# Squares of raw weight blocks moved within a token tile, and the last pair's output products put off for four halves instead of three

## The chip, the cores and the metric

The kernel runs on one core of one Trainium2 chip. The metric is the device time of one execution in microseconds. Three runs of the kernel before gave 1804.94, 1809.9 and 1811.93 us; their median, 1809.9 us, is the time before. The profiled execution of it took 1808.81 us, with a span of 1807.0 us between its first and last instruction.

## The reference, cut to what matters

```python
h = _layernorm(x) * (1 + ca) + sa
x = x + ga * _A_ref(h, ...)              # state space layer, first 450 us of the kernel
h = _layernorm(x) * (1 + cb) + sb
# _B_ref, gated MLP: S = 2048 tokens, D = 576, Fh = 2304
z  = gelu(h @ w_in)                      # (S, 2*Fh)
z1 = z[..., :Fh]
z2 = _layernorm(z[..., Fh:])
g  = einsum("ts,sf->tf", w_sp, z2) + b_sp[:, None]
x  = x + gb * ((z1 * g) @ w_out)         # w_out: (Fh, D)
```

All matrix products are made in parts of half precision: a factor is scaled by a power of two, rounded to a high part, and its remainder is kept as a low part; three products of these parts (high by high, high by low, low by high) are added in PSUM. The scales come from the sums of squares of the raw weights. That is what the squares in this change are for.

## The kernel before, in words

**First part (to about 440 us).** The state space layer `ssm`. The change doesn't touch it.

**Phase A (`phase_a`, about 440 to 702 us).** Sixteen tiles of 128 tokens, called token tiles here, b = 0 to 15. Each makes the second half of z: five groups of 14 matmuls (`z2_mm`, columns 512h to 512h+511) into PSUM tiles `pz`, gelu on ScalarE (`z2_gelu`), the statistics on VectorE (`z2_stats`, `roots`), the normalization on ScalarE (`z2_norm`, one tile late), and a store to DRAM from GpSimd (`z2_store`). The z tile has two buffers, so the first gelu of tile b waits until the store of tile b-2 has landed. The transposed rows `nt` of the next tile are split by ScalarE (`turn_hi`) and VectorE (`turn_lo`); TensorE starts a tile when its `nt` is there.

Every engine here keeps the order in which the code is written. The main work stands in that order by hand, and side work is hung into it: `side(b, k, fn, ...)` puts a call at place k of tile b. The places that matter are, in the order of one tile: LD (loads, at the start), A0 (ScalarE, after the first group of matmuls and ahead of the first gelu of the tile), PE, V0, A1 (after the third gelu, ahead of the fourth), V1 (ahead of the last group). The side work is

- `side_load`, `side_sum`, `side_hi`, `side_lo`: the first half of w_in, one column block q in two token tiles; its sum of squares stands at A0 of the odd tiles, and a small matmul at PE (`win_scale`) needs it.
- `wsp_load`, `out_load`: raw blocks of w_sp and w_out (26 in all, two in a tile, 512 KB or 432 KB each) into the tile `wsst`, which has two buffers; `norm_sp`, `norm_out`: ScalarE squares such a block in place and adds up the squares into a column of `acc`. A load into a buffer waits until the block before in it has been squared.
- from tile 9 on, `block_load`, `wsp_sums`, `wsp_hi`, `wsp_lo`: blocks 0 to 6 of w_sp for the first output quarter, through a single buffer `xz`: load at V1 of a tile, sums on VectorE at V0 of the next, high parts on ScalarE at A1, low parts on VectorE at V1, then the next load into the buffer.

In the code before, the loads of a pair of raw blocks stand at A1 of tile b, and their squares at A0 of tile b+1.

**Phase B (`phase_b`, about 702 us to the end).** Four quarters q of 512 output tokens. In each, 18 units of z1 (`z1_unit`), nine units of g (`g_unit`, f = 0 to 8; `g_products` runs 168 matmuls into four PSUM banks, VectorE combines them into `gt`, multiplies with z1, and ScalarE and VectorE split the product into `prods[q, f]`), then `out_block(q)`. For q < 3 the eight w_sp blocks of the next quarter are built ahead of `out_block` in the code (`wsp_build`: four subtractions L1001 to L1004 and two low parts L787 on VectorE, two high parts L781 on ScalarE, for each block). Here VectorE, ScalarE and TensorE are not held to the written order: when the program is built, a scheduler sets the order of each engine's queue by its own estimates, and the order stays fixed after that.

`out_block(q)` makes eight halves (tt, h): 128 tokens by 288 columns, called h0 to h7 below. Each takes two of the eight PSUM banks, `pa` and `pl`, and adds over nine f and two k, three matmuls each: 54 matmuls, six of them for f = 8. Since `prods[q, 8]` comes last, h0, h1 and h2 first run f = 0 to 7, 48 matmuls each; then the six of f = 8 follow for each of the three. `out_sum` empties a half: ScalarE reads `pl` into `ot` (L1431), VectorE adds `pa` (L1432), multiplies (L1433) and adds the residual rows (L1434). h4 is the first half that takes banks which an earlier half has used.

Of the kernel before, what the change touches and what calls it, by code (L numbers as in the profile page):

```python
# [752 lines left out]
class Mlp:  # L753
# [418 lines left out]
    def phase_a(self):  # L1172
# [13 lines left out]
        LD, PE, A0, A1, V0, V1 = range(6)  # L1186
        sides = [[[] for _ in range(6)] for _ in range(17)]

        def side(b, k, fn, *a):
            sides[b][k].append((fn, a))  # L1190
# [13 lines left out]
        for h in range(2):  # L1204
            side(1, LD, self.bsp_load, ap, h)
            side(2, A0, self.norm_bsp, h)
        for i in range(8):
            side(2 + i // 2, A1, self.wsp_load, 0, i, ap)
            side(3 + i // 2, A0, self.norm_sp, 0, i)
        for i in range(12):  # L1210
            side(6 + i // 2, A1, self.out_load, ap, i)
            side(7 + i // 2, A0, self.norm_out, i)
        for i in range(6):
            side(12 + i // 2, A1, self.wsp_load, 1, i, ap)
            side(13 + i // 2, A0, self.norm_sp, 1, i)
        side(13, V1, self.sums_out)
        side(14, PE, self.scales_out)
        side(6, V1, self.sums_sp, 0)
# [217 lines left out]
    def out_block(self, q):  # L1436

        nc = self.nc
        A, S = nc.scalar, nc.sync
        halves = [(tt, h) for tt in range(4) for h in range(2)]  # L1440
        xts, pms = {}, {}
        for n, (tt, h) in enumerate(halves):
            if h == 0:
                xts[tt] = self.raw(("x", tt)).rearrange("p k n -> p (k n)")[:, :D]
                S.dma_start(xts[tt], self.x1_d[4 * q + tt])
            pms[tt, h] = [self.bank()[:, :288] for _ in range(2)]
            self.out_products(pms[tt, h], q, tt, h, range(8) if n < 3 else range(9))
            for k in range(3) if n == 2 else () if n < 2 else (n,):
                tt, h = halves[k]
                if n == 2:  # L1450
                    self.out_products(pms[tt, h], q, tt, h, (8,))
                self.out_sum(pms[tt, h], xts[tt], q, h)
                b, hs = 4 * q + tt, slice(288 * h, 288 * h + 288)
                if b == 15:
                    (A, S)[h].dma_start(self.out[b, :, hs], xts[tt][:, hs])
                elif h == 1:
                    A.dma_start(self.out[b], xts[tt])
# [170 lines left out]
```

## Time and profile before

| what | value |
|---|---|
| median of 3 runs | 1809.9 us (1804.94 to 1811.93) |
| profiled execution | 1808.81 us, span 1807.0 us |
| TensorE (PE) busy | 1696.9 us, 94% of the span |
| VectorE (DVE) busy | 1120.0 us, 62% |
| ScalarE (ACT) busy | 786.0 us, 43% |
| mean granted TensorE clock | 0.984 of full |

PE, DVE, ACT, POOL and SP are the engines TensorE, VectorE, ScalarE, GpSimd and SyncE. A row of the timeline gives start, duration, engine, source line, operation, output and inputs; brackets at its end give the idle time of that engine just before it, and what ended it. Instructions of phase A all carry the line of the helper that records them, L129, and are told apart by their tiles. A busy PE is one with a matmul in flight; matmuls overlap, so a matmul of 0.29 us can start 0.12 us after the one before it.

### The profile page before, as it was taken

What the parts mean: (1) busy time and instruction counts of PE and PEld (TensorE: products, weight loads), DVE (VectorE), ACT (ScalarE), POOL (GpSimd) and SP (SyncE); (2) the same over time, 40 slices, a digit from 0 to 9 for tenths busy, and PEclk for the clock granted to TensorE, in tenths of its full rate; (3) what the DMA queues carried; (4) which work ended last, traced back from release to release, by engine and by line L of the source; (5) the groups of instructions that cost most, each with busy time, mean ns of one, the idle gap of its engine ahead of it and who ended that gap; (6) DMA issues with size and microseconds to landing.
All of it is one profiled execution on the core that took longest, in us unless ns stands there. A gap on an engine that the chain in (4) does not pass through costs nothing.

```text
span 1807.0 us, 34140 instructions
## 1 busy us (share of the span) xinstructions
PE 1696.9 (94%) x14226; PEld 1198.7 (66%) x14226; DVE 1120.0 (62%) x2240; ACT 786.0 (43%) x1021; POOL 227.4 (13%) x358
## 2 busy tenths in 40 slices
PE   3768899997899999999999999999999999999998
PEld 1334555565455544877777778777788777887787
DVE  5787999966988997999685443474222365222322
ACT  3758999944566666555442222242111132011110
POOL 3121222332122211000000000000000000000000
PEclk9988999998999999999999999999999999999999
DMA  7565736679688788887563766572655572455520
GB/s 215 164 183 199 205 110 168 184 205 295 203 259 265 243 247 237 300 291 268 187 228 111 268 243 220 195 262 95 216 187 204 179 263 68 168 181 180 198 82 27
DMA packets 160122, 361.57 MB, mean 200 GB/s; under 512 B 23040, under 2 KB 76800, under 8 KB 158816
## 3 DMA queue, kind: packets, MB, share of 16 engines
q1 hardware_dynamic: 118944, 166.75, 30.4%
q0 software_dynamic: 33536, 155.05, 25.6%
q10 hardware_dynamic: 7488, 37.60, 5.1%
q8 instruction: 111, 1.82, 0.4%
q14 instruction: 43, 0.35, 0.1%
HBM read 256.86 MB, written 93.05 MB: 194 GB/s over the span
## 4 chain that ended last, share of the span: by engine, by line
PE 49%; DVE 17%; DMA 9%; issue 4%; ACT 3%; POOL 0%; SPq 0%; ACTq 0%; DVEq 0%; POOLq 0%
PE ps L1338 9%; PE ps L1373 8%; PE ps L1375 8%; PE ps L1374 8%; PE ps L1422 3%; PE ps L1424 3%; PE ps L1423 3%; DVE zset L1057 3%; DMA raw<-in_w_spT 3%; DVE gt L1387 2%; DMA z_d<-z 2%; PE pz L129 2%; DVE bsz L129 1%; DMA gbs<-in_w_out 1%; ACT z L129 1%
## 5 line engine op out<-in xcount | busy, mean ns | idle before, releaser
L1373 PE MATMUL ps<-wsp,zset 128*128 128x256 f16 x2016 | 550.7, 273 | 2.4 <-DVE gt L1387 2.4
L1375 PE MATMUL ps<-wsp,zset 128*128 128x256 f16 x2016 | 550.8, 273 | 1.1 <-DVE zset L1057 1.1
L1374 PE MATMUL ps<-wsp,zset 128*128 128x256 f16 x2016 | 550.6, 273 | 0.0
L129 PE MATMUL pz<-wz,nt 128*128 128x512 f16 (+1 forms) x1120 | 226.4, 362 | 10.5 <-ACT nt L129 4.5
L1387 DVE SCALAR_TENSOR_TENSOR gt<-ps,sc,bsp 128x512 f32<-128x512 f32 x36 | 27.0, 749 | 316.9 <-PE ps L1375 316.8
L1338 PE MATMUL ps<-n2q,wf 128*128 128x512 f16 x1008 | 223.1, 379 | 0.0
L1373 PEld LDWEIGHTS <-zset 128*128 128x128 f16 x2016 | 197.7, 98 | 29.1 <-DVE gt L1387 2.7
L1374 PEld LDWEIGHTS <-zset 128*128 128x128 f16 x2016 | 197.5, 98 | 26.5
L1375 PEld LDWEIGHTS <-zset 128*128 128x128 f16 x2016 | 197.5, 98 | 24.5 <-DVE zset L1057 1.4
L129 PEld LDWEIGHTS <-nt 128*128 128x128 f16 x1120 | 109.9, 99 | 118.5 <-issue 7.7
L1350 POOL DMA_DIRECT2D zset<-set_d x96 | 50.8, 529 | 972.1 <-PE ps L1375 758.9
L1338 PEld LDWEIGHTS <-wf 128*128 128x128 f16 x1008 | 98.6, 98 | 111.8
L1343 ACT ACTIVATE z<-ps,sc 128x512 f32<-128x512 f32 x56 | 37.8, 680 | 281.4 <-PE ps L1338 278.9
L1423 PE MATMUL ps<-wout,z 128*128 128x288 f16 x448 | 128.3, 286 | 0.1
L1424 PE MATMUL ps<-wout,z 128*128 128x288 f16 x448 | 128.3, 286 | 0.0
L1422 PE MATMUL ps<-wout,z 128*128 128x288 f16 x448 | 128.3, 286 | 0.0
L1387 DVE SCALAR_TENSOR_TENSOR gt<-ps,sc,gt 128x512 f32<-128x512 f32 (+1 forms) x180 | 122.0, 695 | 5.4
L1057 DVE TENSOR_TENSOR zset<-raw,zset 128x1024 f16<-128x1024 f32 x48 | 58.6, 1221 | 73.2 <-ACT zset L1056 73.2
L1056 ACT ACTIVATE zset<-raw 128x1024 f16<-128x1024 f32 x48 | 50.3, 1051 | 99.8 <-PE ps L1375 72.4
L129 ACT ACTIVATE z<-pz,sc 128x512 f32<-128x512 f32 (+1 forms) x80 | 49.8, 644 | 50.9 <-DMA z_d<-z 37.9
L1432 DVE TENSOR_TENSOR ot<-ot,ps 128x288 f32<-128x288 f32 x32 | 14.2, 453 | 82.7 <-ACT ot L1431 82.7
L1431 ACT ACTIVATE ot<-ps 128x288 f32<-128x288 f32 x32 | 12.7, 407 | 108.5 <-PE ps L1422 93.1
(310 smaller groups left out, 2854.7 us busy)
## 6 DMA issues: line engine op xcount, KB each, us to landing
zset<-set_d POOLq DMA_DIRECT2D x96, 896.0 KB, 4.9
set_d<-zset ACTq DMA_DIRECT2D x36, 896.0 KB, 5.9
raw<-z_d SPq DMA_DIRECT2D x48, 512.0 KB, 4.6
wf<-win_d SPq DMA_DIRECT2D x72, 320.0 KB, 3.4
raw<-in_w_spT SPq DMA_DIRECT2D x43, 512.0 KB, 6.3
z_d<-z POOLq DMA_DIRECT2D x32, 576.0 KB, 7.9
u_d<-st1o POOLq DMA_DIRECT2D x16, 576.0 KB, 3.9
u<-u_d SPq DMA_DIRECT2D x36, 256.0 KB, 5.2
```

The costliest lines, as they stand in the source:

```text
L129: return self.tc.keep_in_program_order(f(*a, **k))
L1056: nc.scalar.activation(o[:, k, 0], t, AF.Copy)
L1057: nc.vector.tensor_tensor(o[:, k, 1], t, o[:, k, 0], op=ALU.subtract)
L1338: nc.tensor.matmul(pm.rearrange("p (t c) -> p t c", t=4), w[:, kw], self.n2[q][:, :, kn], start=i == 0, stop=i == len(Z1) - 1)
L1350: self.nc.gpsimd.dma_start(o, self.set_d[n // 4, n % 4])
L1373: T.matmul(pm, z[:, a, 0, c], w[:, b, 0], start=i + half == 0, stop=False, skip_group_check=True)
L1374: T.matmul(pm, z[:, a, 0, c], w[:, b, 1], start=False, stop=False, skip_group_check=True)
L1375: T.matmul(pm, z[:, a, 1, c], w[:, b, 0], start=False, stop=i == 7, skip_group_check=True)
L1387: V.scalar_tensor_tensor(dst, pm, inv, to, op0=ALU.mult, op1=ALU.add)
L1422: T.matmul(pl, p[:, 1, ts], w[:, 0, hs], start=st, stop=sp)
L1423: T.matmul(pa, p[:, 0, ts], w[:, 0, hs], start=st, stop=False)
L1424: T.matmul(pa, p[:, 0, ts], w[:, 1, hs], start=False, stop=sp)
```

## The change

Two edits. In phase A the squares (`norm_sp`, `norm_out`) go from A0 of the token tile to A1 of the same tile, and are registered ahead of the loads, so that on ScalarE they follow the third gelu of a tile and stand ahead of `wsp_hi`, and each load is issued after the squares that free its buffer. In `out_block` four halves, h0 to h3, run f = 0 to 7 first; then f = 8 follows for these four. No instruction is added or taken away; the queues of GpSimd and SyncE keep their order.

```diff
@@ phase_a
         for i in range(8):
+            side(3 + i // 2, A1, self.norm_sp, 0, i)
+        for i in range(12):
+            side(7 + i // 2, A1, self.norm_out, i)
+        for i in range(6):
+            side(13 + i // 2, A1, self.norm_sp, 1, i)
+        for i in range(8):
             side(2 + i // 2, A1, self.wsp_load, 0, i, ap)
-            side(3 + i // 2, A0, self.norm_sp, 0, i)
         for i in range(12):
             side(6 + i // 2, A1, self.out_load, ap, i)
-            side(7 + i // 2, A0, self.norm_out, i)
         for i in range(6):
             side(12 + i // 2, A1, self.wsp_load, 1, i, ap)
-            side(13 + i // 2, A0, self.norm_sp, 1, i)
@@ out_block
             pms[tt, h] = [self.bank()[:, :288] for _ in range(2)]
-            self.out_products(pms[tt, h], q, tt, h, range(8) if n < 3 else range(9))
-            for k in range(3) if n == 2 else () if n < 2 else (n,):
+            self.out_products(pms[tt, h], q, tt, h, range(8) if n < 4 else range(9))
+            for k in range(4) if n == 3 else () if n < 3 else (n,):
                 tt, h = halves[k]
-                if n == 2:
+                if n == 3:
                     self.out_products(pms[tt, h], q, tt, h, (8,))
                 self.out_sum(pms[tt, h], xts[tt], q, h)
```

## The prediction

> **What bounds the kernel now.** I read the page first (busy shares, and the chain that ended last), then busy time by stretches, then TensorE's idle times and the timelines of ScalarE and VectorE around them.
>
> ```profile
> PE 1696.9 (94%) x14226; PEld 1198.7 (66%) x14226; DVE 1120.0 (62%) x2240; ACT 786.0 (43%) x1021; POOL 227.4 (13%) x358
> ...
> PE 49%; DVE 17%; DMA 9%; issue 4%; ACT 3%; POOL 0%; SPq 0%; ACTq 0%; DVEq 0%; POOLq 0%
> ```
> ```profile
> 487.00:605.00 118.00, 117.60 (x628) 61.84 (x627) 104.48 (x329) 80.37 (x123) 29.52 (x40) 1.00 0.78 250
> 605.00:702.00 97.00, 91.71 (x476) 46.81 (x475) 85.10 (x251) 63.50 (x89) 18.66 (x22) 0.98 0.81 247
> ```
> ```profile
> 960.00:1190.00 230.00, 230.00 (x1842) 179.93 (x1840) 101.17 (x163) 60.48 (x79) 11.63 (x22) 1.00 0.60 215
> ```
>
> The columns of the stretches are length, then busy time of PE, PEld, DVE, ACT and POOL. TensorE is the bound in the quarters of phase B (230.00 of 230) and in phase A up to tile 8 (117.60 of 118). From tile 9 on it is 5.3 us idle out of 97, and VectorE, 85.10 us busy there before the small gaps between its instructions are counted, sets the pace. So whatever makes TensorE wait in phase B is paid in full, and in the second half of phase A what delays VectorE is paid.
>
> **The output blocks.** TensorE's rows around the f = 8 products of the first three quarters; each stall ends with the last split of `prods[q, 8]` (L1403), and the rows without brackets are the last matmul ahead of the first stall and the second matmul of h4:
>
> ```profile
> 944.90 0.29 PE L1424 MATMUL ps<-wout,z1b 128*128 128x288 f16 x1
> 946.66 0.30 PE L1422 MATMUL ps<-wout,z1b 128*128 128x288 f16 x1 [1.47 <-ACT z1b L1403]
> ...
> 955.61 0.29 PE L1423 MATMUL ps<-wout,z 128*128 128x288 f16 x1
> ...
> 1219.97 0.30 PE L1422 MATMUL ps<-wout,z1b 128*128 128x288 f16 x1 [0.63 <-ACT z1b L1403]
> ...
> 1228.92 0.29 PE L1423 MATMUL ps<-wout,z 128*128 128x288 f16 x1
> ...
> 1494.49 0.30 PE L1422 MATMUL ps<-wout,z1b 128*128 128x288 f16 x1 [1.61 <-ACT z1b L1403]
> ...
> 1503.44 0.29 PE L1423 MATMUL ps<-wout,z 128*128 128x288 f16 x1
> ```
>
> What the edit removes: three waits, 1.47 + 0.63 + 1.61 = 3.7 us. With h3's 48 matmuls put in, TensorE reaches f = 8 some 5.9 us later than now (48 at 0.1226; from 946.66 to 955.61 are 73 starts), well after `prods` is there. In the last quarter there is no such stall and nothing to win.
>
> What it adds: h4 comes closer to the sums that free its banks. Before, between f = 8 of h0 and the start of h4 lay the 54 matmuls of h3, 6.6 us; after, only the f = 8 products of h1 to h3, 18 matmuls or 2.2 us. The sums of h0 wait in queues that hold w_sp builds. First ScalarE, then VectorE:
>
> ```profile
> 953.87 0.69 ACT L1431 ACTIVATE ot<-ps 128x288 f32<-128x288 f32 x2
> 956.28 1.15 ACT L781 ACTIVATE wsp<-sum,sc 128x1024 f16<-128x1024 f32 x1 [1.72 <-DVE sum L1004]
> ...
> 1229.59 1.15 ACT L781 ACTIVATE wsp<-sum,sc 128x1024 f16<-128x1024 f32 x1 [1.72 <-DVE sum L1004]
> ...
> 1504.11 1.15 ACT L781 ACTIVATE wsp<-sum,sc 128x1024 f16<-128x1024 f32 x1 [1.72 <-DVE sum L1004]
> ```
> ```profile
> 955.83 0.42 DVE L1004 TENSOR_TENSOR sum<-raw,sum 128x256 f32<-128x256 f32 x1
> 956.16 0.81 DVE L1432 TENSOR_TENSOR ot<-ot,ps 128x288 f32<-128x288 f32 x2
> ...
> 957.63 1.28 DVE L787 SCALAR_TENSOR_TENSOR wsp<-sum,sc,wsp 128x1024 f16<-128x1024 f32 x1
> ...
> 959.82 0.46 DVE L1432 TENSOR_TENSOR ot<-ot,ps 128x288 f32<-128x288 f32 x1 [0.17 <-ACT ot L1431]
> ```
>
> Before, ScalarE's two reads of `pl` (953.87) stand ahead of the last build (956.28); h4 takes the two `pl` banks that these reads free, at 954.56, and starts at 955.49 without waiting. In the order of the changed program both engines do the last build first: on ScalarE the last high part precedes all L1431, on VectorE the last low part L787 precedes the first L1432. And h4 takes `pl` and `pa` of h0, so its second matmul waits for VectorE's L1432. The time of that is fixed by VectorE, which is busy with builds without a break and sees nothing of the edit before this point: L1004 ends and releases ScalarE's last high part at 956.28 as now; this ends at 957.43; then L787 takes 1.28, to 958.71; then L1432 takes 0.46, to 959.17. TensorE's second matmul of h4 starts there instead of at 955.61: 3.6 us later. In the second quarter 1229.59 + 1.15 + 1.28 + 0.46 = 1232.48 against 1228.92, 3.6; in the third 1504.11 + 2.89 = 1507.00 against 1503.44, 3.6. This is net of the removed waits: **+10.7 us**. The last quarter has no builds in these queues; there h0's sums need 1.15 us (0.69 for two L1431, 0.46 for L1432) against 2.2 us of cover, so nothing. Cover gone, this would cost the 3.6 a fourth time.
>
> The new stall itself is 3.6 plus the old wait: 5.1, 4.2 and 5.2 us. Stalls of this length have a second price:
>
> ```profile
> 883.83 0.28 PE L1373 MATMUL ps<-wsp,zset 128*128 128x256 f16 x1 [2.38 <-DVE gt L1387]
> ```
> ```profile
> 885.40:888.80 3.40, 3.40 (x20) 2.48 (x18) 3.33 (x5) 0.69 (x1) 0.00 (x0) 0.54 0.82 319
> 888.80:893.00 4.20, 4.20 (x41) 3.77 (x39) 3.11 (x5) 2.08 (x3) 0.00 (x0) 1.00 0.23 96
> 945.00:950.00 5.00, 3.53 (x30) 2.68 (x29) 5.00 (x11) 2.75 (x3) 0.00 (x0) 1.00 0.19 59
> ```
>
> After an idle time of 2.38 us the granted clock (the column before the DMA share) fell to 0.54 for 3.4 us, in which 20 matmuls started; at the pace of the next stretch, 41 in 4.2 us, it would have been 33. The 13 missing cost 13 x 0.102 = 1.3 us; a whole such stretch at half rate costs 1.7. The stall of 1.47 us at 946.66 left the clock at 1.00. I take 1.6 us for each of three stalls, **+4.8 us**, nearest to the 2.38 us row. Bounds: nothing, if the dip falls inside the stall, and two stretches each, 3.2 x 3 = 9.6.
>
> The Trainium skill ("TensorE: Matmul & The Clock Gate", Part 1) has the clock halved only after at least one idle window of about 3.4 us of a free-running grid. By it a stall of 5.2 us holds a whole window in about half of its placements, and as an estimate from that page the three would cost about 2 us instead of 4.8. The row above speaks against it: 2.38 us, shorter than such a window, was enough here.
>
> **The squares.** Per tile ScalarE's work is the same; its place moves from a spot where ScalarE mostly waits anyway into the dense middle.
>
> ```profile
> ACT z L129 <- DMA z_d<-z: 37.9, 11, 6.6
> ```
> ```profile
> 625.45 1.80 ACT L129 ACTIVATE wsp<-xz,sc 128x1792 f16<-128x1792 f32 x1
> ...
> 670.96 1.80 ACT L129 ACTIVATE wsp<-xz,sc 128x1792 f16<-128x1792 f32 x1
> ...
> 674.96 1.06 ACT L129 ACTIVATE wsst<-wsst 128x1024 f32<-128x1024 f32 x1 [1.26 <-DMA wsst<-in_w_spT]
> ...
> 680.25 1.06 ACT L129 ACTIVATE wsst<-wsst 128x1024 f32<-128x1024 f32 x1 [4.15 <-DMA wsst<-in_w_spT]
> ...
> 700.76 1.78 ACT L129 ACTIVATE wsp<-xz,sc 128x1792 f16<-128x1792 f32 x1
> ```
> ```profile
> 628.65 2.03 DVE L129 SCALAR_TENSOR_TENSOR wsp<-xz,sc,wsp 128x1792 f16<-128x1792 f32 x1
> ...
> 672.98 2.08 DVE L129 SCALAR_TENSOR_TENSOR wsp<-xz,sc,wsp 128x1792 f16<-128x1792 f32 x1
> ...
> 685.25 1.10 DVE L129 TENSOR_TENSOR xz<-xz 128x256 f32<-128x256 f32 x3 [4.51 <-DMA xz<-in_w_spT]
> ...
> 702.57 2.08 DVE L129 SCALAR_TENSOR_TENSOR wsp<-xz,sc,wsp 128x1792 f16<-128x1792 f32 x1 [0.20 <-ACT wsp L129]
> ```
>
> What it removes: squares no longer hold ScalarE ahead of a tile's first gelu while their load is late (1.26 and 4.15 us in front of tile 14), and the loads, issued later in a tile, let the z2 store go first; ScalarE waits 37.9 us for such stores. Little of that is on the path from tile 9 on, where VectorE sets the pace. What it adds: `wsp_hi` comes two squares, 2 x 1.06 = 2.1 us, later, and VectorE's `wsp_lo` waits for it. In tile 10, `wsp_hi` ends at 627.25 and would end at 629.2 (the blocks of w_out are a little shorter), against 628.65: 0.6 us; tile 12 the same; tile 13, 672.8 + 2.1 = 674.9 against 672.98: 2.0. These 3.2 us run into VectorE's wait of 4.51 us for the `xz` load, where the load's slow landing beside the raw loads can take them up. Behind it, tile 14 pays up to 2.1, of which I count half, since ScalarE is no longer held until 681 ahead of that tile; tile 15 pays its 2.2 in full, as VectorE waits there for `wsp_hi` already. VectorE's delay passes to TensorE in the first quarter: the 2.38 us stall above, ended by VectorE, says that TensorE has no slack against it. I take 1.1 + 2.2 = **+3.3 us**. The upper bound counts 3.2 + 2.1 + 2.1 = 7.4; the lower is a gain, bounded by TensorE's waits of that stretch and the dip after the longest:
>
> ```profile
> PE pz L129 <- ACT nt L129: 3.8, 4, 2.1
> PE pz L129 <- DVE nt L129: 1.5, 1, 1.5
> ```
>
> 3.8 + 1.5 + 1.7 = 7.0 us. SyncE's later loads (w_in column blocks, `x1_load`) stand behind the raw loads and go later with them; they are used about a tile later (the 118.00 us stretch above is eight tiles, so 14.7 us), which hides it.
>
> **Sum.** 10.7 + 4.8 + 3.3 = 18.8 us on the profiled execution of 1808.81 us: 1827.6. That execution lies 1.1 us under the median; I predict **1828 us**.
>
> **Rivals.**
> - *The clock mostly holds.* Only one of the three stalls brings a dip that TensorE's work meets, the others none or one that ends inside the stall: 10.7 + 1.6 + 3.3 = 15.6, 1824 us. For it: 1.47 us left the clock alone. Against: 2.38 didn't. 0.13. The rule of the Trainium skill named above would lead here.
> - *Phase A gains what the output blocks lose.* The store waits and the late squares were what held ScalarE's `nt`, and with them gone all 7.0 us of TensorE's loss goes: 15.5 - 7.0 = 8.5, 1817 us. For it: 37.9 us of waiting; against: VectorE's queue has no room. 0.12.
> - *Phase A loses more.* The squares in tiles 4 and 6 push the w_in sums behind them, on which TensorE's scale matmuls wait (some 2 us), and all 7.4 us on VectorE are paid: 15.5 + 9.4 = 25, 1834 us. 0.11.
> - *Faster.* The banks of h4 come free in time: then 3.7 us of waits go at no price and up to 7.0 in phase A: 1798 us. It decides at L1432 of h0 ending before 953.9 (945.02 plus 72 matmuls); the queue orders put it at 959.2. 0.04.
>
> The forecast keeps 0.60.
>
> **How the numbers follow.** 0.5% of 1809.9 is 9 us, about what a measurement of this kernel can tell from no change. Slower by more: forecast, first and third rival, 0.84; within: second, 0.12; faster: 0.04. The low end, 1815, holds the second rival; the high end, 1837, is the three upper bounds together, 10.7 + 9.6 + 7.4 = 27.7. Both signs hardly meet here, so one range stands.
>
> **What would show it.** In the changed profile: no wait for L1403 in front of the f = 8 products; instead, in three quarters, a wait of 4 to 5 us in h4's first two matmuls, ended by L1432 or L1431; granted clock near 0.5 for some 3.4 us behind it; two squares between third and fourth gelu of a tile, and longer waits of VectorE for `wsp_hi` in tiles 13 to 15. I am wrong if h4 starts without a wait, or if phase A ends over 4 us earlier.

## The result and the profile after

| kernel | median | profiled execution | span | granted clock |
|---|---|---|---|---|
| before | 1809.4 us (4 runs, 1804.94 to 1811.93) | 1808.81 us | 1807.0 us | 0.984 |
| changed | 1832.8 us (4 runs, 1831.74 to 1833.97) | 1832.74 us | 1830.7 us | 0.979 |

The ratio is 1.0131, 95% interval 1.0106 to 1.0157: slower by 23.7 us (19.2 to 28.4), where 18.8 us were forecast. The predicted time was 1828, the range 1815 to 1837.

The page of the changed kernel: the busy line, and the groups of out matmuls that wait (busy us, mean ns; idle us before them and what ended it). The second and third lines of `out_products` are L1425 and L1426 now, and `out_sum` begins at L1434.

```profile
PE 1705.5 (93%) x14226; PEld 1201.5 (66%) x14226; DVE 1121.9 (61%) x2240; ACT 784.9 (43%) x1021; POOL 228.0 (12%) x358
...
L1425 PE MATMUL ps<-wout,z 128*128 128x288 f16 x448 | 129.6, 289 | 10.2 <-ACT ot L1434 10.2
L1426 PE MATMUL ps<-wout,z 128*128 128x288 f16 x448 | 129.7, 289 | 3.5 <-DVE ot L1435 3.2
```

10.2 + 3.2 us are new waits for the sums of the output halves; the waits for the last split of `prods[q, 8]` are gone.

Where the time went can be read from six marks. First, the timeline of the kernel before (on TensorE the five transposes that turn the rows of tile 2, which stand in tile 1; the first z2 store on GpSimd, the first matmul of phase B, the first and the last out matmul of the first quarter), then the same of the changed kernel, with the first and last out matmul of the last quarter.

```profile
486.83 0.71 PE L129 MATMUL pt<-ident,n 128*128 128x128 f32 x5
489.65 2.03 POOL L129 DMA_DIRECT2D z_d<-z  x2 [14.17 <-ACT z L129]
702.32 7.93 PE L1338 MATMUL ps<-n2q,wf 128*128 128x512 f16 x36
927.38 0.29 PE L1422 MATMUL ps<-wout,z 128*128 128x288 f16 x1
981.83 0.29 PE L1424 MATMUL ps<-wout,z1b 128*128 128x288 f16 x1
```
```profile
480.49 0.71 PE L129 MATMUL pt<-ident,n 128*128 128x128 f32 x5
485.93 2.04 POOL L129 DMA_DIRECT2D z_d<-z  x2 [14.16 <-ACT z L129]
707.42 2.75 PE L1341 MATMUL ps<-n2q,wf 128*128 128x512 f16 x12
936.53 0.29 PE L1425 MATMUL ps<-wout,z 128*128 128x288 f16 x1
996.39 0.29 PE L1427 MATMUL ps<-wout,z1b 128*128 128x288 f16 x1
...
1772.86 0.29 PE L1425 MATMUL ps<-wout,z 128*128 128x288 f16 x1
1825.66 0.29 PE L1427 MATMUL ps<-wout,z1b 128*128 128x288 f16 x1
```

| stretch | before | changed | difference |
|---|---|---|---|
| start to the first z2 store | 489.65 | 485.93 | -3.7 |
| first z2 store to phase B | 212.67 | 221.49 | +8.8 |
| phase B to the first out matmul | 225.06 | 229.11 | +4.1 |
| out block, first quarter | 54.45 | 59.86 | +5.4 |
| out blocks, second, third, last quarter | 53.60, 54.80, 52.79 | 56.80, 60.03, 52.80 | +8.4 |
| the three stretches between the blocks, and the end | 663.98 | 664.68 | +0.7 |
| span | 1807.0 | 1830.7 | +23.7 |

The first row isn't the edit's: no square moves before tile 3, and over the profiles of this study the first store lies between 485.7 and 490.1 us, the turn of tile 2 between 480.1 and 486.8. The output blocks cost 13.8 us. What phase A costs depends on the mark, since the first store is made by another engine than the rest, and a loss of phase A can also show behind it: the third stretch takes 223.4 to 229.1 us in these profiles. Counted on TensorE alone, from the turn to the first out matmul, the four profiles in which phase A isn't edited (before, experiments 1, 3 and 8) agree: 440.55, 441.61, 441.39 and 440.05 us. The changed kernel has 456.04. By this count the squares cost 15.5 us in this execution, and its earlier turn (480.49 against 486.83) gives 6.3 back. Of the 15.5 us TensorE loses 1.3 up to the turn of tile 6 and 7.9 from there to the turn of tile 8, then 2.2 up to phase B and 4.1 in phase B.

**Output blocks.** TensorE at the start of h4, all three stalls; then ScalarE and VectorE around the first:

```profile
966.90 0.40 PE L1425 MATMUL ps<-wout,z 128*128 128x288 f16 x1 [3.75 <-ACT ot L1434]
968.29 0.40 PE L1426 MATMUL ps<-wout,z 128*128 128x288 f16 x1 [0.99 <-DVE ot L1435]
...
1245.95 0.28 PE L1425 MATMUL ps<-wout,z 128*128 128x288 f16 x1 [2.58 <-ACT ot L1434]
1247.34 0.28 PE L1426 MATMUL ps<-wout,z 128*128 128x288 f16 x1 [1.10 <-DVE ot L1435]
...
1524.31 0.28 PE L1425 MATMUL ps<-wout,z 128*128 128x288 f16 x1 [3.90 <-ACT ot L1434]
1525.69 0.40 PE L1426 MATMUL ps<-wout,z 128*128 128x288 f16 x1 [1.10 <-DVE ot L1435]
```
```profile
965.41 1.15 ACT L781 ACTIVATE wsp<-sum,sc 128x1024 f16<-128x1024 f32 x1 [2.32 <-DVE sum L1004]
966.46 0.69 ACT L1434 ACTIVATE ot<-ps 128x288 f32<-128x288 f32 x2
```
```profile
966.59 1.28 DVE L787 SCALAR_TENSOR_TENSOR wsp<-sum,sc,wsp 128x1024 f16<-128x1024 f32 x1 [1.22 <-ACT wsp L781]
967.79 0.45 DVE L1435 TENSOR_TENSOR ot<-ot,ps 128x288 f32<-128x288 f32 x1
```

Each stall comes in two pieces: the read of `pl` frees the bank of the first matmul, L1435 that of the second, and each stands right behind the last build on its engine. The stalls are 4.7, 3.7 and 5.0 us. A block without any wait takes 52.80 us (last quarter: 1825.66 - 1772.86). The first has 59.86 - 52.80 = 7.06, so 2.3 us beside its stall; the second 4.00, 0.3 beside; the third 7.23, 2.2 beside. Most of that rest is the clock; 0.2 to 0.4 us of it the blocks of the kernel before, too, have beside their waits (54.45 - 52.80 - 1.47 = 0.18), and the third holds a wait of 0.34 us for `gt`. Two stretches after the first stall and one after the second (length; busy us and starts of PE, PEld, DVE, ACT, POOL; granted clock; DMA share; GB/s):

```profile
966.90:970.00 3.10, 2.11 (x9) 1.17 (x9) 3.03 (x7) 0.67 (x2) 0.00 (x0) 0.50 0.47 182
970.00:973.50 3.50, 3.50 (x22) 2.39 (x21) 2.89 (x7) 0.41 (x1) 0.00 (x0) 0.69 0.24 89
1245.90:1249.40 3.50, 2.35 (x18) 1.75 (x18) 3.43 (x8) 0.71 (x2) 0.00 (x0) 1.00 0.44 161
```

Read in steps of half a us, the clock fell while TensorE still stood in the first stall, at about 965.4, and was back at about 972.2: 6.8 us at half rate, 5.3 of them behind the first matmul of h4. Around the second stall it stayed at 1.00. At the third it fell at about 1525.1, for 3.4 us.

**Phase A.** TensorE's waits for the sums of w_in in tiles 5 and 7:

```profile
535.71 0.38 PE L129 MATMUL pz<-acc,ones 128*128 128x1 f32 x2 [1.17 <-ACT wso L129]
...
569.45 0.59 PE L129 MATMUL pz<-acc,ones 128*128 128x1 f32 x2 [5.01 <-ACT wso L129]
```

The same two matmuls in the kernel before:

```profile
540.73 0.38 PE L129 MATMUL pz<-acc,ones 128*128 128x1 f32 x2
...
569.86 0.38 PE L129 MATMUL pz<-acc,ones 128*128 128x1 f32 x2 [0.40 <-ACT wso L129]
```

What the wait in tile 7 is for, in the changed kernel on ScalarE and on SyncE, and SyncE of the kernel before:

```profile
549.78 1.06 ACT L129 ACTIVATE wsst<-wsst 128x1024 f32<-128x1024 f32 x1
...
566.97 2.34 ACT L129 ACTIVATE wso<-wst 128x2560 f16<-128x2560 f32 x1 [2.39 <-DMA wst<-in_w_in]
```
```profile
550.96 1.40 SPq L129 DMA_DIRECT2D wsst<-in_w_spT  x2
552.41 2.66 SPq L129 DMA_DIRECT2D wst<-in_w_in  x3
```
```profile
545.91 0.90 SPq L129 DMA_DIRECT2D wsst<-in_w_spT  x2
546.86 2.21 SPq L129 DMA_DIRECT2D wst<-in_w_in  x3
```

On SyncE the w_in load stands behind the raw loads. These now wait for the squares that free `wsst`, the first of which ends at 550.84; so the w_in load goes out at 552.41 instead of 546.86. It lands 12.7 us later, the sum of squares waits 2.39 us for it, TensorE 5.01 us for the sum, and then runs at a clock of 0.50 for two stretches of 3.4 us.

Measured against TensorE's own progress the load is later than that. It went out 6.1 us behind the scale matmul of tile 5 before (546.86 - 540.73) and goes out 16.7 us behind it now (552.41 - 535.71). TensorE was ready for the sum of tile 7 at 569.46 before and at 564.44 now. So the load had 22.6 us, and now has 12.0, less than the transfer alone takes.

From tile 9 on, VectorE's waits (in total, times, longest) and three of them in the timeline:

```profile
DVE xz L129 <- DMA xz<-in_w_spT: 8.7, 3, 5.1
DVE wsp L129 <- ACT wsp L129: 5.7, 5, 2.7
```
```profile
610.11 1.56 DVE L129 TENSOR_TENSOR xz<-xz 128x256 f32<-128x256 f32 x4 [2.21 <-DMA xz<-in_w_spT]
...
678.79 2.08 DVE L129 SCALAR_TENSOR_TENSOR wsp<-xz,sc,wsp 128x1792 f16<-128x1792 f32 x1 [1.75 <-ACT wsp L129]
...
711.63 2.08 DVE L129 SCALAR_TENSOR_TENSOR wsp<-xz,sc,wsp 128x1792 f16<-128x1792 f32 x1 [2.74 <-ACT wsp L129]
```

The forecast waits for `wsp_hi` in tiles 13 and 15 are there at 1.75 and 2.74 us (forecast 2.0 and 2.2). A wait for `xz` in tile 9, 2.21 us, is new and was not forecast. TensorE itself waits for ScalarE's `nt` from tile 11 on, 6.0 us in all against 3.8 before. ScalarE's waits for the z2 stores grew from 37.9 us to 60.6, the longest of them 8.4.

### The profile page after: what moved, and what is told of

The parts are those of the page before. It is cut to its first block, busy times and chain, and to the rows that moved or that the text cites. A ratio compares the mean times of both kernels' runs of the same rounds, so it can differ in the third digit from the quotient of the medians.

```text
span 1830.7 us, 34114 instructions
## 1 busy us (share of the span) xinstructions
PE 1705.5 (93%) x14226; PEld 1201.5 (66%) x14226; DVE 1121.9 (61%) x2240; ACT 784.9 (43%) x1021; POOL 228.0 (12%) x358
## 4 chain that ended last, share of the span: by engine, by line
PE 44%; DVE 16%; DMA 10%; issue 8%; ACT 4%; SPq 1%; POOL 0%; ACTq 0%; DVEq 0%; POOLq 0%
PE ps L1341 9%; PE ps L1376 8%; PE ps L1378 8%; PE ps L1377 8%; DVE zset L1057 3%; PE ps L1426 2%; DMA z_d<-z 2%; PE ps L1427 2%; PE ps L1425 2%; DMA raw<-in_w_spT 2%; DVE gt L1390 2%; PE pz L129 1%; DVE wsp L787 1%; ACT z L129 1%; DMA wst<-in_w_in 1%
## 5 line engine op out<-in xcount | busy, mean ns | idle before, releaser
L129 PE MATMUL pz<-wz,nt 128*128 128x512 f16 (+1 forms) x1120 | 229.1, 364 | 10.9 <-ACT nt L129 6.7
L1390 DVE SCALAR_TENSOR_TENSOR gt<-ps,sc,bsp 128x512 f32<-128x512 f32 x36 | 26.9, 748 | 317.0 <-PE ps L1378 316.8
L129 PEld LDWEIGHTS <-nt 128*128 128x128 f16 x1120 | 110.7, 100 | 120.7 <-issue 10.6
L1425 PE MATMUL ps<-wout,z 128*128 128x288 f16 x448 | 129.6, 289 | 10.2 <-ACT ot L1434 10.2
L1426 PE MATMUL ps<-wout,z 128*128 128x288 f16 x448 | 129.7, 289 | 3.5 <-DVE ot L1435 3.2
L1427 PE MATMUL ps<-wout,z 128*128 128x288 f16 x448 | 129.6, 289 | 0.0
L129 ACT ACTIVATE z<-pz,sc 128x512 f32<-128x512 f32 (+1 forms) x80 | 49.6, 644 | 69.4 <-DMA z_d<-z 60.6
L1435 DVE TENSOR_TENSOR ot<-ot,ps 128x288 f32<-128x288 f32 x32 | 14.4, 451 | 92.4 <-ACT ot L1434 92.4
L1434 ACT ACTIVATE ot<-ps 128x288 f32<-128x288 f32 x32 | 12.8, 408 | 120.6 <-PE ps L1425 110.2
```

The source lines that it names most:

```text
L129: return self.tc.keep_in_program_order(f(*a, **k))
L1390: V.scalar_tensor_tensor(dst, pm, inv, to, op0=ALU.mult, op1=ALU.add)
L1425: T.matmul(pl, p[:, 1, ts], w[:, 0, hs], start=st, stop=sp)
L1426: T.matmul(pa, p[:, 0, ts], w[:, 0, hs], start=st, stop=False)
L1427: T.matmul(pa, p[:, 0, ts], w[:, 1, hs], start=False, stop=sp)
```

## The experiments

Each was timed in five rounds beside the kernel before on its chip, whose median was 1805.2 (runs 1 to 4), 1806.1 (5 to 8) and 1806.2 us (9 to 11). Ratios are of the same chip, with 95% intervals; microseconds are the ratio times 1805. A profile is one execution: those of 2, 5 and 6 lie 7.5, 3.3 and 4.6 us under the median of their kernel and that of 9 lies 4.3 above, so their rows show which waits there are, and the medians what an edit costs.

**1. The output blocks' edit alone.** The second hunk of the diff, not the first:

```diff
-range(8) if n < 3 else range(9)
+range(8) if n < 4 else range(9)
-for k in range(3) if n == 2 else () if n < 2 else (n,):
+for k in range(4) if n == 3 else () if n < 3 else (n,):
```

> The output blocks' edit alone (four halves put off), the squares as before. My theory: three stalls of h4 on the sums of h0, net 3.6 us each after the removed waits for L1403, and dips of the clock of about 3.4 us in all (2.0 + 0 + 1.4, from the matmuls that ran at half rate in the changed kernel): 1809.4 + 10.7 + 3.4 = 1823.5 us, range 1820 to 1826, and phase A as in the kernel before (220 us from the first w_in scale group of tile 1 to the start of phase B). Rival 'the squares are harmless, the output blocks cost it all': 1833. Rival 'the loss sits in phase A': under 1815.

Ratio 1.0100 (1.0086 to 1.0115), +18.1 us (15.5 to 20.8). Phase A is 209.1 us, not longer than before. The three stalls are 4.9, 4.2 and 4.9 us. The second, and the first stretch behind it:

```profile
1233.46 0.40 PE L1422 MATMUL ps<-wout,z 128*128 128x288 f16 x1 [3.22 <-ACT ot L1431]
1234.85 0.40 PE L1423 MATMUL ps<-wout,z 128*128 128x288 f16 x1 [0.99 <-DVE ot L1432]
```
```profile
1233.40:1236.80 3.40, 2.35 (x10) 1.31 (x10) 3.33 (x7) 0.72 (x3) 0.00 (x0) 0.50 0.46 164
```

Here the second stall halved the clock too, from about 1232.4 to 1239.2. The blocks take 60.11, 59.57 and 60.31 us by their first and last matmuls; less 52.80 and less the stalls, the rest is 2.4, 2.6 and 2.6 us, 7.6 in all. My expectation had taken over the spared dip of the changed kernel and came out 4 us low; the median lies inside its stated 1820 to 1826, with a faster kernel before on this chip.

**2. The squares' edit alone.** The first hunk, not the second (shown for one of three groups of blocks):

```diff
-            side(7 + i // 2, A0, self.norm_out, i)
+            side(7 + i // 2, A1, self.norm_out, i)    # ahead of the loads
```

> The squares' edit alone, three halves put off as before. My theory: phase A is some 9.75 us longer (229.95 against 220.2 in the two profiles), of which about 5 us in tiles 5 to 7, where TensorE's scale group of w_in waits for ScalarE's sum and that for the late w_in load, and about 4.5 us from tile 9 on, where VectorE waits for wsp_hi behind the squares: 1809.4 + 9.5 = 1819 us, range 1815 to 1822. The waits for L1403 are as before. Rival 'the squares are harmless': 1809. The prediction's own term: 1812.7.

Ratio 1.0049 (1.0037 to 1.0061), +8.8 us (6.7 to 11.0), as expected. The wait in tile 7 is there, in this run 3.25 us long:

```profile
566.89 0.58 PE L129 MATMUL pz<-acc,ones 128*128 128x1 f32 x2 [3.25 <-ACT wso L129]
```

**3. Two builds behind the sums.** Experiment 1, with the last two builds emitted after the sums of h0 to h3, and these sums and builds held to the written order on ScalarE and VectorE:

```diff
-                for i in range(8):
+                for i in range(6):
                     self.wsp_build(q + 1, i)
@@ out_block, after the sums of h0 to h3
+            if n == 3 and q < 3:
+                for i in range(6, 8):
+                    self.wsp_build(q + 1, i)
```

> The output blocks' edit alone, with the last two builds of w_sp (i = 6 and 7) put behind the sums of h0 to h3 on ScalarE and VectorE. My theory (h4 waits for its banks because the sums of h0 queue behind these builds): L1432 of h0 ends at about 962, just when TensorE is through with the f = 8 products of h3; no stall, no dip, and the three removed waits of 3.7 us stay won: 1809.4 - 3.7 = 1805.7 us, range 1803 to 1809. Rival 'h4 would stall anyway, by the latency of the sums themselves': 1817 to 1823. Rival 'the builds are then late for the next quarter's products': a new wait of the g products for L787, over 1815.

Ratio 0.9984 (0.9971 to 0.9996): 2.9 us faster than before (0.7 to 5.2). The blocks take 52.80, 52.80, 53.33 and 52.80 us: no stall of h4, no dip (the third holds a wait of 0.36 us for `gt`). The cause of the stall is the queue of builds in front of the sums; experiment 8 separates it from the written order, which this one fixes at the same time.

**4. The squares' edit, with the w_in load ahead.**

```diff
-            side(2 * q, LD, self.side_load, q)
+            if q == 0:
+                side(0, LD, self.side_load, 0)
+            else:
+                side(2 * q - 1, A1, self.side_load, q)
```

> The squares' edit alone, with SyncE's load of the next w_in column block put ahead of the raw loads of the tile before instead of behind them. Theory 'the late load': in the changed kernel the load of tile 6 goes out at 552.4 instead of 546.9 us because it stands behind raw loads that wait for the squares; with it early, the 5.0 us wait of TensorE in tile 7 and its 2.9 us of half clock go, 5 to 6.5 us in all: 1813 to 1814 us. Rival 'ScalarE is late by the squares themselves or by the z_d stores it waits for': the wait in tile 7 stays within 1 us of that of the squares' edit alone, 1819 us.

Ratio 1.0023 (1.0011 to 1.0035), +4.2 us: 4.6 us less than in experiment 2. SyncE sends the w_in load ahead of the raw loads that wait:

```profile
542.20 1.90 SPq L129 DMA_DIRECT2D wst<-in_w_in  x3
550.60 1.68 SPq L129 DMA_DIRECT2D wsst<-in_w_spT  x2
```

From 540 to 600 us TensorE waits 0.3 us for the sums of w_in. The squares stand where they stood in experiment 2, so their place on ScalarE did not make the wait in tile 7; the late load did. The wait in tile 5, at 538.14, is 1.91 us in this profile and did not go.

**5. In addition, the raw loads behind the load of `xz`.** Experiment 4, with the loads of raw blocks at V1, behind `block_load`:

```diff
-            side(6 + i // 2, A1, self.out_load, ap, i)
+            side(6 + i // 2, V1, self.out_load, ap, i)
```

> The squares' edit with the w_in load ahead (as in the run before) and, in addition, the raw loads put behind the w_sp block load (xz) of the same tile on SyncE. Theory 'the xz load is late behind the raw loads': VectorE's new wait of 2.2 us for xz in tile 9 goes and the one of 4.1 us in tile 14 shrinks; 2 us less than with the w_in load ahead alone, so about 2 us above the kernel before (+0.1%). Rival 'xz's lateness is covered or set by xz's own buffer': no change, +0.23%. Rival 'the raw loads are then late for their squares': ScalarE waits for wsst, over +0.3%.

Ratio 1.0035 (1.0022 to 1.0049). No gain. VectorE's waits for `xz` fell from 7.2 to 4.2 us, those for `wsp_hi` rose from 5.2 to 7.5.

**6. The squares behind `wsp_hi`.** Experiment 4, with squares and raw loads registered behind `wsp_hi`:

```diff
-            side(7 + i // 2, A1, self.norm_out, i)
             side(9 + i, A1, self.wsp_hi, 0, i)
+            side(7 + i // 2, A1, self.norm_out, i)
```

> The squares' edit with the w_in load ahead, and the squares (with the raw loads behind them) put behind wsp_hi in the tile instead of ahead of it. Theory 'wsp_hi is late by two squares and VectorE pays': VectorE's waits for wsp_hi (0.35 + 0.36 + 1.80 + 2.74 = 5.2 us) go, of which some 3 to 4 us reach TensorE: about the time of the kernel before (0.0 to +0.1%). Rival 'the squares hold ScalarE's gelus and splits wherever they stand in the middle of the tile': no change, +0.23%.

Ratio 1.0023 (1.0008 to 1.0039). No gain: the waits for `wsp_hi` are gone altogether, and the waits for `xz` rose from 7.2 to 11.6 us:

```profile
DVE xz L129 <- DMA xz<-in_w_spT: 11.6, 4, 6.1
```

In experiments 4, 5 and 6 the two waits add up to 12.4, 11.7 and 11.6 us, where the kernel before has 6.6. Taking one away lengthens the other.

**7. The w_in load ahead, nothing else.** The diff of experiment 4 on the kernel before.

> The kernel before with the w_in load ahead of the raw loads and nothing else. It tells whether the gain of 4.7 us by that load belongs to the squares' edit. My theory: in the kernel before the w_in load is not held by squares on SyncE and lands in time, so nothing changes: within 0.1% of the kernel before. Rival 'an early w_in load is worth some us in any case': 3 to 5 us faster.

Ratio 1.0021 (1.0005 to 1.0038): slower by 3.8 us (0.9 to 6.9), which neither theory expected. With squares at A0, ahead of the first gelu, ScalarE now waits for the raw loads that the w_in load pushed back, 22.0 us against 5.7 before, and TensorE for ScalarE's `nt`, 6.9 us against 3.8:

```profile
ACT wsst L129 <- DMA wsst<-in_w_spT: 22.0, 6, 5.5
```

So the early load is no gain by itself, and the 4.6 us of experiment 4 are not a general one. Against this kernel the squares' edit costs nothing that can be measured (1.0023 against 1.0021).

**8. Only the last build behind the sums.** As experiment 3, with i = 7 alone:

```diff
-                for i in range(6):
+                for i in range(7):
                     self.wsp_build(q + 1, i)
```

> The output blocks' edit alone with only the last build (i = 7) behind the sums of h0 to h3. If the stall is the queue of builds, it shrinks by what one build takes: from the rows of the changed kernel, the low part of build 6 then ends about 964.3 us and L1432 of h0 at 964.8, against TensorE ready at 962.9: stalls of about 1.9, 1.2 and 2.0 us instead of 4.7, 3.7 and 5.0. Against the kernel before: 5.1 - 3.7 = +1.4 us if the clock holds through them, and up to 2.5 us more for each stall that lets it drop, so +0.1% to +0.4%.

Ratio 0.9998 (0.9983 to 1.0013). Three shorter stalls, 1.1, 0.7 and 1.5 us, where 1.9, 1.2 and 2.0 were expected:

```profile
951.23 0.28 PE L1423 MATMUL ps<-wout,z 128*128 128x288 f16 x1 [1.10 <-DVE ot L129]
...
1224.63 0.28 PE L1423 MATMUL ps<-wout,z 128*128 128x288 f16 x1 [0.72 <-DVE ot L129]
...
1497.79 0.28 PE L1422 MATMUL ps<-wout,z 128*128 128x288 f16 x1 [0.44 <-ACT ot L129]
1499.17 0.28 PE L1423 MATMUL ps<-wout,z 128*128 128x288 f16 x1 [1.10 <-DVE ot L129]
```

With two builds ahead of the sums the stalls are 4.9, 4.2 and 4.9 us (experiment 1), with one less 1.1, 0.7 and 1.5, with two less none. Sums and moved builds are held to the written order here as in experiment 3, so that order by itself does not remove the stall. The clock held in these; they weigh about as much as the waits that the edit removes (3.4 against 3.7 us), and the time is that of the kernel before.

**9 and 10. The squares' edit in tiles 3 to 8 alone, and from tile 9 on alone.** The place of each square depends on its tile, and in experiment 10 the other way round:

```diff
-            side(7 + i // 2, A1, self.norm_out, i)
+            side(7 + i // 2, A1 if 7 + i // 2 < 9 else A0, self.norm_out, i)
```

> The squares' edit in tiles 3 to 8 alone (8 blocks of w_sp and the first 4 of w_out); from tile 9 on the squares stand where they stood before. Theory 'the late w_in load costs most': TensorE's waits for the w_in sums in tiles 5 and 7 (1.2 to 5.0 us) and the half clock behind the longer one stay, 4 to 6 us, +0.2% to +0.35% of the 0.49% that the whole squares' edit took. Rival 'VectorE's waits from tile 9 on cost it': +0.1% or less.

> The squares' edit from tile 9 on alone (the last 8 blocks of w_out and 6 of w_sp); up to tile 8 the squares stand where they stood before. VectorE's waits for wsp_hi (5.2 us) and xz are then as with the whole edit, TensorE's waits for the w_in sums as before. By the prediction's own term 3.3 us (+0.18%); rival 'the early tiles cost it all': 0.0%; rival 'the late tiles cost it all': +0.45%.

Tiles 3 to 8: 1.0023 (1.0010 to 1.0037), +4.2 us, with a wait of 2.62 us in tile 7. From tile 9 on: 1.0029 (1.0013 to 1.0045), +5.2 us, with no wait for the w_in sums above 0.8 us and 4.9 us of VectorE's waits for `wsp_hi`. Together 9.4 us, where experiment 2 has 8.8: the parts add, within their intervals. In the profile of experiment 10 TensorE takes 446.12 us from the turn of tile 2 to the first out matmul, 4.5 to 6.1 more than the four profiles without the edit, which agrees with the median. Only part of it shows by the start of phase B (217.9 us from the turn, against 214.3 to 216.6). The rest comes in the first quarter, where TensorE's wait for VectorE's `gt` is 4.1 us, against 1.8 to 3.5.

**11. Both edits, both mends** (experiments 3 and 4).

> Both edits, with the two mends of the earlier runs: the last two builds of w_sp behind the sums of h0 to h3, and the w_in load ahead of the raw loads. If the parts add, -0.16% + 0.23% = +0.07%, 1 us above the kernel before, where the two edits alone take +1.31%. Rival 'the two edits cost something together that neither mend touches': over +0.4%.

Ratio 0.9990 (0.9977 to 1.0003): -1.8 us (-4.2 to +0.5). The blocks take 52.99, 52.79, 52.80 and 52.80 us. The whole loss of 1.31% is gone; that this kernel beats the one before is not shown. Experiment 3, without the squares' edit, is the one version here that does.

## Why the prediction was right, and which term was off

**The output blocks (forecast 10.7 + 4.8 = 15.5; measured 13.8 in the profile, 18.1 alone).** The mechanism is shown. The waits for L1403 went; h4's second matmul waited for VectorE's sum of h0, which waited for the last low part, which waited for the last high part (rows above). Stalls forecast at 5.1, 4.2 and 5.2 us measured 4.7, 3.7 and 5.0. Experiments 3 and 8 took the builds out of the way and the stall went in proportion. The last quarter has none, as forecast. Of the clock, three dips of 1.6 us were forecast; the rest beside the stalls is 2.3, 0.3 and 2.2 us in the changed kernel's profile, 4.8 in all, and 7.6 in experiment 1. That the sum met 4.8 us is luck: it is made of two larger dips and none at the second stall, and experiment 1 has all three. The first dip was 6.8 us long, the two stretches of the upper bound and not the one assumed, but 2.5 us of it fell inside the two pieces of the stall.

**The rule on the clock.** The Trainium skill ("TensorE: Matmul & The Clock Gate", Part 1), by which a stall must hold a whole idle window of about 3.4 us, was named beside the rival at 1824 us. Its variation from placement to placement agrees with the runs: 2.58 + 1.10 us left the clock at 1.00, 3.22 + 0.99 us in the same place halved it. That a whole window must be idle does not: 2.15 us were enough in the kernel before (rows in the last section) and 2.62 us in experiment 9, which fell to 0.52.

**The squares (forecast +3.3; measured +8.8 alone, +5.2 from tile 9 on alone, +4.2 before it alone; 15.5 in the changed kernel's profile).** The step that failed is the last sentence of that part: that the loads behind the raw loads on SyncE are "used about a tile later", "which hides it". The w_in load went out 5.55 us later, 10.6 us later by TensorE's progress, and took 12.7 us to land; what covered it shrank from 22.6 to 12.0 us, and TensorE stood for 5.01 us and then ran at half clock. Experiment 4 shows this: the load ahead of the raw loads, with the squares in place, takes the wait and 4.6 us away. The error was to measure the cover from the load's place in the code, and not from its issue to its landing. The DMA issues of the kernel before between 530 and 580 us (KB, us to landing) had the number. With some 2.3 us for the sum of squares it left about 6 of the 22.6 us free, so a load late by less than a tile was enough:

```profile
wst<-in_w_in SPq DMA_DIRECT2D x1, 1024.0 KB, 14.1
```

The rival "phase A loses more" gave 1834 us, nearer to the measured 1832.8 than the forecast. It had the victim right (the w_in sums, TensorE's scale matmuls) and the cause wrong: it blamed the squares on ScalarE. The rival "phase A gains" rested on ScalarE's waits for the z2 stores, and these grew (37.9 to 60.6 us).

The term from tile 9 on, 3.3 us, lies about 2 under the 5.2 of experiment 10, but inside its own bounds and inside that interval (2.3 to 8.1), so that it was too small is not shown. The waits for `wsp_hi` came near their forecast sizes. That VectorE's wait for the `xz` load would take up those of tiles 10 to 13 was wrong: that wait, 4.51 us before, was 5.11 after, and another was added in tile 9. That VectorE's delay reaches TensorE in the first quarter fits the profile of experiment 10.

**The total.** The two edits alone cost 18.1 + 8.8 = 26.9 us, together 23.7, and 18.8 were forecast. That the time came within 5 us of 1828 is in part luck: the loss by the w_in load, which the sum put at nothing, was partly made up by the spared dip. A slip beside it: 1827.6 and the 1.1 us to the median make 1828.7, and the times of the rivals leave the 1.1 us out.

**What stays open.** Experiments 5 and 6 show that VectorE's waits for `wsp_hi` and for `xz` change places, so neither is by itself what costs the 5.2 us; what sets their sum is not settled. Nor is how the 15.5 us of the changed kernel's profile go with the 8.8 us of experiment 2: the wait in tile 7 alone was 5.01, 3.25 and 2.62 us in three kernels that move the squares there (the changed one, experiments 2 and 9).

## What to carry to other kernels

When an edit makes one load in a queue wait, follow every load behind it to its landing and to its user: here a load that had 22.6 us before its user came left only 12.0, and TensorE stopped, because the transfer alone took 12.7. Before more halves are put off, ask which instruction frees the banks of the next one, and what stands ahead of it in its engine's fixed queue; moving two builds behind those sums turned a loss of 18 us into a gain of 3.

## What was not expected of the hardware

The length of a wait did not decide whether TensorE's clock fell. In front of tile 15 the kernel before waited 2.15 us and fell to 0.53, and the same tile's matmuls in the kernel of experiment 8, behind a wait of 2.40 us, ran at 1.00. First the kernel before, the wait and the stretch after it, then experiment 8:

```profile
687.01 15.48 PE L129 MATMUL pz<-wz,nt 128*128 128x512 f16 x70 [2.15 <-ACT nt L129]
```
```profile
686.90:690.30 3.40, 3.29 (x8) 1.17 (x9) 3.34 (x7) 3.40 (x7) 1.88 (x3) 0.53 0.73 198
```
```profile
685.76 13.79 PE L129 MATMUL pz<-wz,nt 128*128 128x512 f16 x70 [2.40 <-ACT nt L129]
```
```profile
685.70:689.20 3.50, 3.44 (x16) 1.58 (x17) 3.25 (x6) 3.50 (x7) 1.82 (x3) 1.00 0.74 202
```

The 70 matmuls of the tile took 15.48 us behind the shorter wait and 13.79 behind the longer one.
